# Attention with decay and a squared-relu feed-forward on one core: the order of all engines from a list scheduler, the first tokens in pairs, free choice of engine, weight quarters between the loads

## The chip, the cores and the metric

One core of one Trainium2 chip. The metric is the device time of one execution in microseconds (us). Engines are named TensorE (PE in the profile; its weight loads are PEld), VectorE (DVE), ScalarE (ACT), GpSimd (POOL) and SyncE (SP, which issues loads and stores here). Runs of one kernel can show steps of 0.6 to 1.7% that mostly, but not always, go with the granted TensorE clock (in one set of runs the kernel before took 218.1 to 218.2 us at 0.989 to 0.991 and 219.5 to 220.0 at 0.983 and 0.984); each comparison below is therefore made between runs taken together, on one chip, and where runs at other times are compared their ratios to the kernel before are used.

## The reference

```python
B, H, S, D = 4, 8, 768, 48          # d_model = H*D = 384, d_ff = 2048
for t in range(S):                   # decayed linear attention
    cur = einsum('bhd,bhe->bhde', u * k[t], v[t])
    y[t] = einsum('bhd,bhde->bhe', r[t], state + cur)
    state = w * state + einsum('bhd,bhe->bhde', k[t], v[t])
x = y as (B*S, H*D)                  # 3072 tokens
g = relu(x @ w_in) ** 2
out = g @ w_out
```

Both kernels cut the 768 steps into six chunks of 128, so that there are 24 *blocks* (chunk by batch) of 128 tokens.

## The kernel before

In the cuts and profiles below, `hps` (`ps_h` in the changed kernel) is a result of the first feed-forward product and `ops` (`ps_o`) one of the second. Per block, attention needs five elementwise *products* of 128x384 (`kpad = k*wk`, `rpad = r*wr`, `rk = r*k`, `rku = rk*u`, `dv = v*du`) and, from the second chunk on, a sixth (`sm*wc`). All run on GpSimd.

```python
def prep(n):
    nc.gpsimd.tensor_tensor(kp[:, :, :D], kt, wk, ALU.mult)       # kpad
    nc.gpsimd.tensor_tensor(rp[:, :, :D], rt, wr, ALU.mult)       # rpad
    nc.scalar.copy(vb, vt)
    nc.gpsimd.tensor_tensor(rk, rt, kt, ALU.mult)
    nc.gpsimd.tensor_tensor(rku, rk, ub, ALU.mult)
def du(n):  nc.vector.tensor_reduce(q["du"], q["rku"], axis=X, op=ALU.add)
def dv(n):  nc.gpsimd.tensor_tensor(q["dv"], q["vb"], du broadcast, ALU.mult)
# s1: transposes of kp, rp -> rkT;  k^T v -> state sm;  state_end: sm *= wc (GpSimd)
# s2: at = k r^T, masked on VectorE -> AT;  s3: y -> yb (VectorE);  s4: transpose -> xt
...
def m1(c, f):                          # one of 16 column tiles of a chunk of four blocks
    for kk in range(NK): nc.tensor.matmul(out=hps, lhsT=w_in_sb[...], rhs=xts[c][:, kk]...)
    nc.vector.tensor_scalar(gr, hps, 0.0, None, ALU.max)                    # relu
    nc.scalar.activation(gs[c][:, f]..., gr, AF.Square)                     # square
def m2(c, b, part):                    # a quarter of one block's second product
    for f in range(part * 4, part * 4 + 4): nc.tensor.matmul(out=ops, lhsT=gs[c][:, f, b, :], rhs=w_out_sb[:, f, :], ...)
    ...
for slot in range(-2, NU + 2 * B):     # the fixed order
    at(slot + 1, dv); at(slot + 2, prep)
    if slot == 1: all four w_in quarters are loaded
    if 3 <= slot < 7: one w_out quarter is loaded
    at(slot + 1, s1); moe(0); at(slot, s3); moe(1)
    at(slot + 1, state_end); at(slot + 1, s2); moe(2); at(slot, s4); moe(3)
    at(slot + 2, du); load(slot + 5)
    # moe(part): m1 of the chunk one behind, m2 of the chunk two behind
```

Of the kernel before, what the change touches and what calls it, by code (L numbers as in the profile page):

```python
# [15 lines left out]
def kernel(  # L16
# [23 lines left out]
    NU = NCH * B  # L40

    const = ctx.enter_context(tc.tile_pool(name="const", bufs=1))
    lpool = ctx.enter_context(tc.tile_pool(name="loads", bufs=5))
    apool = ctx.enter_context(tc.tile_pool(name="attn", bufs=3))
    xpool = ctx.enter_context(tc.tile_pool(name="xg", bufs=2))
    mpool = ctx.enter_context(tc.tile_pool(name="moe", bufs=4))
    aps = ctx.enter_context(tc.tile_pool(name="attn_psum", bufs=3, space=bass.MemoryType.PSUM))
    hps_pool = ctx.enter_context(tc.tile_pool(name="h_psum", bufs=3, space=bass.MemoryType.PSUM))
    ops_pool = ctx.enter_context(tc.tile_pool(name="o_psum", bufs=2, space=bass.MemoryType.PSUM))
# [7 lines left out]
    wcol = const.tile([128, NP], F32)  # L57
    nc.vector.memset(wcol, 1.0)
    with nc.allow_non_contiguous_dma(reason="384 decay values, one column a head"):
        for i in range(2):  # L60
            nc.scalar.dma_start(
                out=wcol[i * PAD : i * PAD + D, :],
                in_=bass.AP(tensor=w.tensor, offset=w.offset + i * D, ap=[[1, D], [2 * D, NP]]),
            )
    ub = const.tile([128, H, D], F32)
    nc.scalar.dma_start(
        out=ub, in_=bass.AP(tensor=u.tensor, offset=u.offset, ap=[[0, 128], [1, HD]])
    )

    loads = {}  # L70

    def load(n):
        c, b = divmod(n, B)
        t0 = c * C
        tiles = []
        for nm, src in (("kt", k), ("rt", r), ("vt", v)):
            t = lpool.tile([C, H, D], F32, name=nm)
            nc.sync.dma_start(out=t, in_=src[b, :, t0 : t0 + C, :].rearrange("h t d -> t h d"))
            tiles.append(t)
        loads[n] = tiles  # L80

    NAHEAD = 5
    for n in range(NAHEAD):
        load(n)

# [5 lines left out]
    def load_w_in(q):  # L91
        fs = slice(q * dff // 4, (q + 1) * dff // 4)
        nc.gpsimd.dma_start(out=w_in_sb[:, :, fs], in_=w_in_v[:, :, fs])  # L93

    def load_w_out(q):
        fs = slice(q * NF // 4, (q + 1) * NF // 4)
        nc.gpsimd.dma_start(out=w_out_sb[:, fs, :], in_=w_out_v[:, fs, :])


    iota_i = const.tile([128, 1], mybir.dt.int32)  # L100
    nc.gpsimd.iota(iota_i, pattern=[[0, 1]], base=0, channel_multiplier=1)
    er = const.tile([128, 1], F32)
    nc.vector.tensor_scalar(er, iota_i, 1.0, float(-MID), ALU.mult, ALU.add)
    ek = const.tile([128, 1], F32)
    nc.vector.tensor_scalar(ek, iota_i, -1.0, float(MID - 1), ALU.mult, ALU.add)
    identb = const.tile([128, 128], BF16)
    make_identity(nc, identb)
    smask = const.tile([128, 128], F32)
    make_upper_triangular(nc, smask, val=1.0, diag=False)

    NPADS = 3
    rpads, kpads = [], []
    for i in range(NPADS):
        rp = const.tile([C, H, PAD], BF16, name=f"rpad{i}")
        kp = const.tile([C, H, PAD], BF16, name=f"kpad{i}")
        nc.vector.memset(rp, 0.0)
        nc.vector.memset(kp, 0.0)
        rpads.append(rp)
        kpads.append(kp)


    lnw = const.tile([128, HD], F32)
    nc.scalar.activation(lnw, wb, AF.Ln)
    lnc = const.tile([128, NP], F32)
    nc.scalar.activation(lnc, wcol, AF.Ln)
    wk = const.tile([128, H, D], F32)
    nc.scalar.activation(wk.rearrange("p h d -> p (h d)"), lnw, AF.Exp, scale=ek)  # L127
    wr = const.tile([128, H, D], F32)
    nc.scalar.activation(wr.rearrange("p h d -> p (h d)"), lnw, AF.Exp, scale=er)
    wcs = const.tile([128, NP], F32)  # L130
    nc.scalar.activation(wcs, lnc, AF.Exp, scale=float(C))
    wc = const.tile([128, NP, 2, D], F32)
    nc.vector.memset(wc, 0.0)
    for i in range(2):
        rows = slice(i * PAD, i * PAD + D)
        nc.vector.tensor_copy(wc[rows, :, i, :], wcs[rows, :, None].to_broadcast([D, NP, D]))

    states = {b: None for b in range(B)}
    stb = {b: None for b in range(B)}
    xts, gs = {}, {}  # L140
    unit = {}

    def prep(n):
        kt, rt, vt = loads.pop(n)
        rp, kp = rpads[n % NPADS], kpads[n % NPADS]
        nc.gpsimd.tensor_tensor(kp[:, :, :D], kt, wk, ALU.mult)  # L146
        nc.gpsimd.tensor_tensor(rp[:, :, :D], rt, wr, ALU.mult)  # L147
        vb = apool.tile([C, H, D], BF16, name="vb", bufs=4)
        nc.scalar.copy(vb, vt)  # L149
        rk = apool.tile([C, H, D], F32, name="rk")  # L150
        nc.gpsimd.tensor_tensor(rk, rt, kt, ALU.mult)  # L151
        rku = apool.tile([C, H, D], F32, name="rku")
        nc.gpsimd.tensor_tensor(rku, rk, ub, ALU.mult)  # L153
        unit[n] = dict(rp=rp, kp=kp, vb=vb, rku=rku)

    def du(n):
        q = unit[n]
        q["du"] = apool.tile([C, H], F32, name="du")
        nc.vector.tensor_reduce(q["du"], q["rku"], axis=mybir.AxisListType.X, op=ALU.add)  # L159

    def dv(n):
        q = unit[n]
        q["dv"] = apool.tile([C, H, D], F32, name="dv")
        nc.gpsimd.tensor_tensor(q["dv"], q["vb"], q["du"][:, :, None].to_broadcast([C, H, D]), ALU.mult)  # L164

    def s1(n):
        c, b = divmod(n, B)
        q = unit[n]
        rk_p = aps.tile([128, NP, 2, C], BF16, name="rk_p", tag="a")
        kv_p = None  # L170
        if c < NCH - 1:
            kv_p = aps.tile([128, NP, 2, D], F32, name="kv_p", tag="a")
        for p in range(NP):
            nc.tensor.transpose(rk_p[:, p, 1, :], q["kp"][:, 2 * p : 2 * p + 2, :], identb)  # L174
        for p in range(NP):
            nc.tensor.transpose(rk_p[:, p, 0, :], q["rp"][:, 2 * p : 2 * p + 2, :], identb)  # L176
        rkT = apool.tile([128, NP, 2, C], BF16, name="rkT")
        nc.scalar.copy(rkT, rk_p)  # L178
        q["rkT"] = rkT
        q["st"] = stb[b]  # L180
        if kv_p is not None:
            for p in range(NP):
                nc.tensor.matmul(
                    out=kv_p[:, p], lhsT=q["kp"][:, 2 * p : 2 * p + 2, :],
                    rhs=q["vb"][:, 2 * p : 2 * p + 2, :], start=True, stop=True,
                )
            sm = apool.tile([128, NP, 2, D], F32, name=f"sm{b}", bufs=2)
            if c == 0:
                nc.vector.tensor_tensor(sm, kv_p, wc, ALU.mult)
            else:  # L190
                nc.vector.tensor_tensor(sm, kv_p, states[b], ALU.add)
            states[b] = sm

    def state_end(n):
        c, b = divmod(n, B)
        if c == NCH - 1:
            return
        sm = states[b]
        if c > 0:
            nc.gpsimd.tensor_tensor(sm, sm, wc, ALU.mult)  # L200
        sb = apool.tile([128, NP, 2, D], BF16, name=f"sb{b}", bufs=2)
        nc.scalar.copy(sb, sm)
        stb[b] = sb

    def s2(n):
        q = unit[n]
        rkT = q["rkT"]
        at = [aps.tile([128, NP, C], F32, name=f"at_p{i}", tag="a") for i in range(2)]
        for p in range(NP):
            for i in range(2):  # L210
                rows = slice(i * PAD, i * PAD + D)
                nc.tensor.matmul(  # L212
                    out=at[i][:, p, :], lhsT=rkT[rows, p, 1, :], rhs=rkT[rows, p, 0, :],
                    start=True, stop=True,
                )
        AT = apool.tile([128, 2, NP, C], BF16, name="AT")
        for i in range(2):
            nc.vector.tensor_tensor(
                AT[:, i], at[i], smask[:, None, :].to_broadcast([128, NP, C]), ALU.mult
            )  # L220
        q["AT"] = AT

    def s3(n):
        c, b = divmod(n, B)
        q = unit[n]
        y_p = aps.tile([128, NP, 2, D], F32, name="y_p", tag="a")
        for p in range(NP):
            if c > 0:
                nc.tensor.matmul(  # L229
                    out=y_p[:, p], lhsT=q["rkT"][:, p, 0, :], rhs=q["st"][:, p],  # L230
                    start=True, stop=False, skip_group_check=True,
                )
            for i in range(2):
                nc.tensor.matmul(  # L234
                    out=y_p[:, p, i, :], lhsT=q["AT"][:, i, p, :], rhs=q["vb"][:, 2 * p + i, :],
# [49 lines left out]
    def at(n, fn):  # L285
        if 0 <= n < NU:
            fn(n)
# [59 lines left out]
```

## Time and profile before

| | before |
|---|---|
| median time, three runs | 220.02 us (219.78 to 220.11) |
| profiled span | 217.1 us |
| TensorE, VectorE, ScalarE, GpSimd busy | 174.7, 133.2, 120.5, 135.4 us |
| first feed-forward matmul (hps) | 45.3 us |

The first fence is from the page of the kernel before: busy time of each engine, then its span in 40 slices, with the busy share of a slice in tenths.

```profile
PE 174.7 (80%) x1480; PEld 101.9 (47%) x1480; DVE 133.2 (61%) x224; ACT 120.5 (55%) x219; POOL 135.4 (62%) x153
...
PE   0135543467578499998999989999999999999993
...
DVE  4245551429758588887787887787777775555200
...
POOL 2488898997996949787888779687687200000000
```

The averages hide two stages. In the first third GpSimd has 8s and 9s while TensorE has 3s to 7s; from about 75 us (slice 14) TensorE has 9s. The next fence is the windows view of the kernel before: for each stretch its length, then busy us (and instructions) of each engine, the granted clock, the DMA share and GB/s.

```profile
core 0: us, PE busy (x) PEld busy (x) DVE busy (x) ACT busy (x) POOL busy (x), PEclk, DMA share, GB/s
20.00:40.00 20.00, 10.04 (x100) 6.88 (x97) 9.37 (x17) 6.73 (x11) 18.28 (x21) 1.00 1.00 175
40.00:60.00 20.00, 12.11 (x108) 6.53 (x106) 11.98 (x22) 8.81 (x17) 18.12 (x21) 1.00 0.99 168
...
80.00:100.00 20.00, 20.00 (x189) 11.99 (x188) 16.40 (x27) 13.72 (x26) 16.11 (x18) 1.00 0.50 107
...
120.00:140.00 20.00, 19.40 (x179) 11.56 (x177) 15.62 (x27) 13.63 (x26) 15.95 (x18) 1.00 0.53 116
```

From 20 to 60 us GpSimd is busy for 36.4 of 40 us, TensorE for 22. From 80 us TensorE is full. The chain of waits of the kernel before (start, length, who) says what one block costs in the first stage:

```profile
9.60 1.01 POOL rpad_137 L147
10.60 0.98 POOL rk L151
...
11.65 1.00 POOL rku L153
...
12.68 0.56 DVE du L159
...
13.37 0.83 POOL dv L164
14.20 0.95 POOL kpad_142 L146
```

Five products on GpSimd and one wait for `du` make 5.5 us a block. The group of such a product, from the page (busy us and mean ns of one after the bar), follows:

```profile
L151 POOL TENSOR_TENSOR rk<-rt,kt 128x384 f32<-128x384 f32 x24 | 23.9, 997 | 0.0
```

### The profile page before, as it was taken

The numbers are of one execution on the slowest core, as the hardware profiler recorded it, in microseconds if no ns is written. First come the engines' busy times: TensorE is split into PE (matmuls) and PEld (weight loads), VectorE is DVE, ScalarE is ACT, GpSimd is POOL, SyncE is SP. The second block draws the span as 40 slices with busy tenths as digits, with TensorE's granted clock in tenths as the row PEclk, the third lists the DMA queues.
The fourth block names the chain that finished last, engine by engine and source line by source line (L and its number), as shares of the span: only waits on it lengthen the run. The fifth ranks groups of instructions, "written<-read, shape, count | busy, mean of one in ns | idle before, by whom it ended". The sixth has DMA issues, their size and how long they took to land.

```text
span 217.1 us, 3956 instructions
## 1 busy us (share of the span) xinstructions
PE 174.7 (80%) x1480; PEld 101.9 (47%) x1480; DVE 133.2 (61%) x224; ACT 120.5 (55%) x219; POOL 135.4 (62%) x153
## 2 busy tenths in 40 slices
PE   0135543467578499998999989999999999999993
PEld 0123332324334255565566655665555555555551
DVE  4245551429758588887787887787777775555200
ACT  3544441057268565866677666866767655555410
POOL 2488898997996949787888779687687200000000
PEclk9999999999979999999999999999999999999998
DMA  5999969999665006346652565536610100111022
GB/s 101 195 199 209 202 119 191 208 175 179 124 104 72 3 0 145 73 100 120 149 120 69 105 145 118 120 78 126 145 41 36 36 35 15 53 48 38 36 72 72
DMA packets 82771, 22.67 MB, mean 104 GB/s; under 512 B 75840, under 2 KB 82752, under 8 KB 82752
## 3 DMA queue, kind: packets, MB, share of 16 engines
q1 hardware_dynamic: 78480, 19.08, 41.1%
q0 software_dynamic: 3712, 3.15, 9.7%
q10 hardware_dynamic: 560, 0.20, 0.4%
q8 instruction: 11, 0.18, 0.3%
q14 instruction: 8, 0.07, 0.1%
HBM read 20.84 MB, written 4.72 MB: 118 GB/s over the span
## 4 chain that ended last, share of the span: by engine, by line
PE 65%; POOL 23%; ACT 3%; DVE 3%; DMA 2%; issue 2%; POOLq 0%; ACTq 0%
PE ops L275 29%; PE hps L259 26%; POOL rku L153 4%; POOL rk L151 4%; POOL dv L164 3%; DMA wcol<-in_w_dram 2%; PE y_p L234 2%; DVE du L159 1%; PE y_p L229 1%; PE rk_p L176 1%; PE rk_p L174 1%; POOL w_in_sb L93 1%; POOL rpad_137 L147 1%; POOL rpad_145 L147 1%; POOL rpad_141 L147 1%
## 5 line engine op out<-in xcount | busy, mean ns | idle before, releaser
L259 PE MATMUL hps<-xt,w_in_sb 128*128 128x512 bf16 x288 | 80.5, 389 | 8.1 <-ACT xt L252 8.1
L265 DVE TENSOR_SCALAR gr<-hps 128x512 f32<-128x512 f32 x96 | 65.8, 688 | 33.7 <-PE hps L259 24.2
L275 PE MATMUL ops<-w_out_sb,g 128*128 128x384 bf16 x384 | 75.5, 326 | 0.0
L266 ACT ACTIVATE g<-gr 128x512 bf16<-128x512 f32 x96 | 59.8, 632 | 27.2 <-DVE gr L265 26.6
L275 PEld LDWEIGHTS <-g 128*128 128x128 bf16 x384 | 37.5, 98 | 33.4
L164 POOL TENSOR_TENSOR dv<-vb,du 128x384 f32<-128x384 bf16 x24 | 19.9, 829 | 26.8 <-DVE du L159 25.2
L259 PEld LDWEIGHTS <-w_in_sb 128*128 128x128 bf16 x288 | 23.8, 99 | 25.0 <-issue 9.9
L178 ACT COPY rkT<-rk_p 128x1024 bf16<-128x1024 bf16 x24 | 24.4, 1015 | 7.3 <-PE rk_p L176 7.3
L153 POOL TENSOR_TENSOR rku<-rk,ub 128x384 f32<-128x384 f32 x24 | 23.9, 996 | 1.9
L159 DVE TENSOR_REDUCE du<-rku 128x8 f32<-128x384 f32 x24 | 13.1, 547 | 18.0 <-POOL rku L153 17.8
L151 POOL TENSOR_TENSOR rk<-rt,kt 128x384 f32<-128x384 f32 x24 | 23.9, 997 | 0.0
L239 DVE TENSOR_TENSOR yb<-y_p,dv 128x384 bf16<-128x384 f32 x24 | 13.3, 554 | 6.1 <-PE y_p L234 6.1
L281 ACT COPY osb<-ops 128x384 f32<-128x384 f32 x24 | 11.2, 466 | 7.9 <-PE ops L275 6.4
L212 PEld LDWEIGHTS <-rkT 48*128 48x128 bf16 x192 | 6.5, 101 | 18.6 <-ACT rkT L178 9.6
L149 ACT CAST vb<-vt 128x384 bf16<-128x384 f32 x24 | 12.3, 513 | 2.3 <-DMA vt<-in_v_dram 2.3
L234 PEld LDWEIGHTS <-AT 128*128 128x128 bf16 x192 | 10.5, 103 | 5.5 <-issue 4.4
L252 ACT COPY xt<-yt_p 128x384 bf16<-128x384 bf16 x24 | 11.1, 462 | 2.1 <-PE yt_p L251 2.1
L234 PE MATMUL y_p<-vb,AT 128*128 128x48 bf16 x192 | 12.1, 191 | 0.0
L146 POOL TENSOR_TENSOR kpad_138<-kt,wk 128x384 bf16<-128x384 f32 x8 | 8.0, 996 | 6.7 <-ACT wk L127 6.7
L174 PE MATMUL rk_p<-identb,kpad_138 128*128 128x128 bf16 x32 | 3.5, 240 | 10.3 <-POOL kpad_138 L146 9.7
L251 PE MATMUL yt_p<-identb,yb 128*128 128x128 bf16 x72 | 8.8, 237 | 0.0
L229 PEld LDWEIGHTS <-rkT 128*128 128x128 bf16 x80 | 7.7, 98 | 1.7 <-issue 0.3
(224 smaller groups left out, 210.7 us busy)
## 6 DMA issues: line engine op xcount, KB each, us to landing
kt<-in_k_dram SPq DMA_DIRECT2D x24, 192.0 KB, 3.5
rt<-in_r_dram SPq DMA_DIRECT2D x24, 192.0 KB, 3.7
vt<-in_v_dram SPq DMA_DIRECT2D x24, 192.0 KB, 3.8
out_dram<-osb SPq DMA_DIRECT2D x24, 192.0 KB, 1.9
w_in_sb<-in_moe_w_in_dram POOLq DMA_DIRECT2D x4, 384.0 KB, 8.6
w_out_sb<-in_moe_w_out_dram POOLq DMA_DIRECT2D x4, 384.0 KB, 5.9
wb<-in_w_dram SPq DMA_DIRECT2D x1, 192.0 KB, 3.6
ub<-in_u_dram ACTq DMA_DIRECT2D x1, 192.0 KB, 5.7
```

The source lines that it names most:

```text
L149: nc.scalar.copy(vb, vt)
L151: nc.gpsimd.tensor_tensor(rk, rt, kt, ALU.mult)
L153: nc.gpsimd.tensor_tensor(rku, rk, ub, ALU.mult)
L159: nc.vector.tensor_reduce(q["du"], q["rku"], axis=mybir.AxisListType.X, op=ALU.add)
L164: nc.gpsimd.tensor_tensor(q["dv"], q["vb"], q["du"][:, :, None].to_broadcast([C, H, D]), ALU.mult)
L178: nc.scalar.copy(rkT, rk_p)
L234: nc.tensor.matmul(out=y_p[:, p, i, :], lhsT=q["AT"][:, i, p, :], rhs=q["vb"][:, 2 * p + i, :], start=(c == 0), stop=True, skip_group_chec ...
L239: nc.vector.tensor_tensor(yb, y_p.rearrange("t p i d -> t (p i d)"), q["dv"].rearrange("t h d -> t (h d)"), ALU.add)
L259: nc.tensor.matmul(out=hps, lhsT=w_in_sb[:, kk, f * 128 : (f + 1) * 128], rhs=xts[c][:, kk].rearrange("p b t -> p (b t)"), start=(kk == 0) ...
L265: nc.vector.tensor_scalar(gr, hps, 0.0, None, ALU.max)
L266: nc.scalar.activation(gs[c][:, f].rearrange("p b t -> p (b t)"), gr, AF.Square)
L275: nc.tensor.matmul(out=ops, lhsT=gs[c][:, f, b, :], rhs=w_out_sb[:, f, :], start=(f == 0), stop=(f == NF - 1),)
```

## The change

The intent is to fill TensorE before 75 us. Every operation becomes an object with its possible engines, assumed durations, dependencies and buffers; a list scheduler repeatedly places the operation that can start first, and the kernel is emitted in that order. Feed-forward starts after two blocks instead of four (pairs for the first four blocks). Products may run on GpSimd or VectorE, relu on VectorE or ScalarE, squares on ScalarE or GpSimd. The weight quarters are issued between the first blocks.

```diff
+    op({"P": 1.0, "V": 0.47}, K + 2, [q["rk"]], two(lambda e, T=T: e.tensor_tensor(T("rku"), T("rk"), ub, ALU.mult)), ...)
+    op({"P": 1.0, "V": 0.47}, K + 0.1, ...)     # kp;  the same for rp, dv ("P": 0.83) and sm*wc; rk on P alone
     [...]
+    groups = [[0, 1], [2, 3]] + [list(range(i, i + B)) for i in range(B, NU, B)]
+    W_IN_AT, W_OUT_AT = (0, 1, 1, 2), (3, 4, 5, 6)
     [...]
+    o_r = op({"V": 0.14 + 0.1375 * L, "A": 0.2 + 0.1 * L}, key - 1, [o_m], relu, uses=[gr, h])
+    o_sq.append(op({"A": 0.22 + 0.1 * L, "P": 0.333 * L}, key - 1, [o_r], square, uses=[gr, g]))
     [...]
+    while left:                                  # the list scheduler
+        for o in left:
+            t = latest end (+ latency) of its dependencies and of the old users of the buffers it takes
+            for e in o.eng:
+                s = max(t, free[e])
+                rank = (s, o.key + (AWAY if e is not the home engine else 0))
+        place the lowest rank; free[e] = s + o.eng[e]
+    for o in placed: o.emit(o.by)
-    for slot in range(-2, NU + 2 * B): [...]     # the fixed order
     [...]
-    wcs = Exp(128 * lnc) on ScalarE              # decay of a chunk, from a one-column load (0.8 KB, 5.0 us)
+    seven times: nc.vector.tensor_tensor(sq, wcs, wcs, ALU.mult)   # 128x4, on VectorE
```

In the schedule that results, 46 of the 136 products are on VectorE (13 `rku`, 10 `kp`, 13 `rp`, 8 `dv`, 2 `sm`), 34 of 112 relus on ScalarE and 27 of 112 squares on GpSimd.

## The prediction

> **What bounds the kernel now.** The span is 217.1 us (median time 220.02, so 2.9 us lie outside it). The chain of waits gives TensorE 65% and GpSimd 23%; the windows show two stages. Until about 72 us GpSimd is the limit (9.1, 9.2, 18.1 us busy in 20-30, 30-40, 40-60), while TensorE has 5 of every 10 us. The chain there runs kpad, rpad, rk, rku, dv at 5.5 us a token block (later 6.5 to 8). The first feed-forward matmul starts at 45.3 us, after four blocks. From 75 us TensorE is full: 6.78 us a block (85.47 to 92.25 in the chain): four hps triples at 0.64, four ops quadruples at 0.65, about 1.6 of attention. The end is 68 ops matmuls (11.2 us) and a 3.5 us tail.
>
> **What the change does.** TensorE work hardly changes (48 hps matmuls of 512 columns become 96 of 256): 6.78 us x 24 blocks, less small parts, is 161 us. The gain must come from filling TensorE before 75 us. The order listing shows:
> - Feed-forward starts after two blocks instead of four; ops matmuls begin in block 5's time instead of block 8's.
> - 46 of 136 attention products go from GpSimd to VectorE; GpSimd gets 27 of 112 squares (20 wide, estimated 1.33 us each from 1.0 for 384 columns); ScalarE takes 34 of 112 relus.
> - My sums from trace durations (moved product estimated 0.5 us): GpSimd 135 -> 125, VectorE 133 -> 146, ScalarE 120 -> 139.
> - Weight quarters are issued from block 0 on, not at 29 us. Loads arrive every 2.9 us a block; the eight quarters took 9.7% of the span, 21 us of all engines. Eight blocks plus weights need about 45 us of DMA either way.
>
> **The sum.** Pair 0's hps start at about 20 us (blocks 0 and 1 through, first quarter landed), 4.5 us of TensorE work done. Then 157 us of it plus 3.5 tail: span 180.5 if never idle. I add:
> - 7 us between 20 and 55, where VectorE, ScalarE and GpSimd together are about 94% loaded (76 of 81 us), weights compete with loads, and TensorE runs at half rate at times. [...] the trace agrees (an hps triple 1.44 us at 45.3, 0.81 at 48.9).
> - 3 us for products on VectorE. [...]
> - 3 us of order misses in the steady part.
>
> The three overlap (some 2.5 us less): span 191, plus 2.9 outside: **194 us** (186 to 204). Faster by over 2%: 0.97; within 2%: 0.025; slower: 0.005.
>
> **What would show it.** First hps at 18-23 us; TensorE near full from 55 us, not 75; block spacing still 6.7-7.0 us there; GpSimd under 70% busy; moved products longer than 0.55 us on average when GpSimd is busy; last tail unchanged.
>
> **What would make it wrong.** [...] the fixed order, built on modelled times, meeting late loads or weights and stalling in-order engines (200+); or the early stage running TensorE full from 25 us (under 187).

The sum came to 194 us: 180.5 if TensorE never idles, plus 7, 3 and 3, less 2.5 of overlap, plus 2.9 outside the span. Two stand as estimates alone: the 3 us, and the part of the 7 us that is slow matmuls. For these "half rate" is the word: the trace of the kernel before shows an hps triple of 1.44 us at 45.3 and one of 0.82 us at 48.9, 1.8 times. The 0.5 us of a moved product is an estimate too; `du` and `yb`, which read 128x384 elements on VectorE, took 0.55 us each in the kernel before.

## The result, and the profile after

| | before | after |
|---|---|---|
| median time, four runs each | 219.9 us (219.75 to 220.11) | 206.27 us (206.07 to 206.49) |
| profiled span | 217.1 us | 204.0 us |
| TensorE, VectorE, ScalarE, GpSimd busy | 174.7, 133.2, 120.5, 135.4 us | 175.2, 153.5, 127.6, 126.3 us |
| mean granted clock | 0.989 | 0.971 |

The ratio is 0.938 (95% interval 0.9363 to 0.9396). Ratios here and below are the mean time of one kernel's fast runs over that of the other's of the same rounds, so not quite the ratio of the medians quoted. The change gained 13.6 us; 26 had been predicted. Busy times and slices, from the page of the changed kernel (PEclk is the granted TensorE clock in tenths):

```profile
PE 175.2 (86%) x1529; PEld 106.4 (52%) x1529; DVE 153.5 (75%) x260; ACT 127.6 (63%) x240; POOL 126.3 (62%) x136
...
PE   0147893999599999977999999799999999999992
...
DVE  4899689478859999899989999999764564455200
...
POOL 2767489548899698999998899995322020422200
PEclk9999999589969999999999999999999999999998
```

TensorE indeed fills earlier. But VectorE, 75% busy in the mean, now has 8s and 9s from slice 12 to slice 27, and TensorE has 7s in the middle of what had been its full stage. The windows view of the changed kernel:

```profile
20.00:40.00 20.00, 14.97 (x125) 10.07 (x127) 15.35 (x29) 11.49 (x28) 13.67 (x18) 0.88 1.13 194
40.00:60.00 20.00, 17.21 (x176) 12.31 (x177) 15.78 (x30) 12.68 (x30) 15.29 (x18) 0.86 0.49 74
...
80.00:100.00 20.00, 17.46 (x179) 10.46 (x177) 19.49 (x33) 15.93 (x30) 19.25 (x19) 1.00 0.96 199
100.00:120.00 20.00, 19.74 (x192) 11.34 (x190) 19.10 (x32) 15.82 (x32) 18.31 (x18) 1.00 0.54 115
120.00:140.00 20.00, 18.88 (x173) 10.81 (x170) 19.97 (x33) 15.80 (x29) 17.93 (x17) 1.00 0.09 32
```

From 80 to 140 us VectorE is busy for 58.6 of 60 us, and TensorE idles for 3.9. The chain of waits of the changed kernel runs through VectorE there:

```profile
87.37 0.50 DVE rku L217
87.86 1.27 DVE kp_79 L220
89.14 0.46 DVE du L228
89.60 0.81 DVE rp_76 L223
...
94.28 1.34 DVE dv L231
```

The pieces differ oddly: `rku` takes 0.50 us and `kp`, of the same size, 1.27. The groups of the changed kernel, by form:

```profile
L214 POOL TENSOR_TENSOR rk<-rt,kt 128x384 f32<-128x384 f32 x24 | 27.3, 1144 | 4.5 <-DVE wsq L171 4.0 <-DVE rku L217 0.5
...
L217 DVE TENSOR_TENSOR rku<-rk,ub 128x384 f32<-128x384 f32 x13 | 9.7, 746 | 0.7 <-POOL rk L214 0.7
...
L231 DVE TENSOR_TENSOR dv<-vb,du 128x384 f32<-128x384 bf16 x8 | 7.8, 971 | 0.2
...
L223 DVE TENSOR_TENSOR rp_75<-rt,wr 128x384 bf16<-128x384 f32 x3 | 5.8, 1932 | 0.0
...
L220 DVE TENSOR_TENSOR kp_79<-kt,wk 128x384 bf16<-128x384 f32 x4 | 3.9, 968 | 0.0
```

Summed over all their groups, the 46 moved products took 44.4 us of VectorE, 0.97 each, almost the 1.0 us that they had cost on GpSimd. `rk`, which stayed on GpSimd, grew from 0.997 to 1.144 us. The timeline of the changed kernel (start, length, engine, operation) shows one of them:

```profile
32.01 0.83 POOL L231 TENSOR_TENSOR dv<-vb,du 128x384 f32<-128x384 bf16 x1
...
32.57 2.59 DVE L223 TENSOR_TENSOR rp_75<-rt,wr 128x384 bf16<-128x384 f32 x1
...
32.80 0.99 POOL L220 TENSOR_TENSOR kp_78<-kt,wk 128x384 bf16<-128x384 f32 x1
...
33.75 0.99 POOL L214 TENSOR_TENSOR rk<-rt,kt 128x384 f32<-128x384 f32 x1
...
35.09 0.55 DVE L321 TENSOR_TENSOR yb<-ps_a,dv 128x384 bf16<-128x384 f32 x1
```

The VectorE product is recorded from 32.57 to 35.16. Three GpSimd products follow each other until 34.74; it ends 0.42 us after the last of them. `yb` behind it, which reads one operand from PSUM, takes 0.55 us.

That product is the extreme. The usual case, from the same view of the same run:

```profile
87.41 1.31 POOL L223 TENSOR_TENSOR rp_75<-rt,wr 128x384 bf16<-128x384 f32 x1
...
87.79 1.35 DVE L220 TENSOR_TENSOR kp_79<-kt,wk 128x384 bf16<-128x384 f32 x1
...
88.68 1.31 POOL L214 TENSOR_TENSOR rk<-rt,kt 128x384 f32<-128x384 f32 x1
```

`kp_79` ends 0.42 us after the GpSimd product that was running, and the next GpSimd product, recorded as starting meanwhile, takes 1.31 us instead of 1.00. Of the 46 moved products 17 took 0.54 to 0.58 us; each of the other 29 ended 0.41 to 0.43 us after a GpSimd operation, and only two of them sat through more than one.

### The profile page after: what moved, and what is told of

Same layout as the page of the kernel before. It is cut to its first block, busy times and chain, and to the rows that moved or that the text cites. A ratio compares the mean times of both kernels' runs of the same rounds, so it can differ in the third digit from the quotient of the medians.

```text
span 204.0 us, 4084 instructions
## 1 busy us (share of the span) xinstructions
PE 175.2 (86%) x1529; PEld 106.4 (52%) x1529; DVE 153.5 (75%) x260; ACT 127.6 (63%) x240; POOL 126.3 (62%) x136
## 4 chain that ended last, share of the span: by engine, by line
PE 66%; DVE 20%; DMA 6%; issue 3%; POOL 3%; ACT 1%; POOLq 0%; DVEq 0%; ACTq 0%
PE ps_o L396 27%; PE ps_h L363 26%; DMA w_out_sb<-in_moe_w_out_dram 4%; PE ps_a L241 4%; DVE AT L298 3%; PE ps_a L288 3%; PE ps_a L313 2%; DMA wrow<-in_w_dram 2%; DVE rku L217 2%; DVE gr L374 2%; PE ps_a L331 2%; PE ps_a L308 2%; DVE dv L231 2%; DVE rp_75 L223 1%; DVE yb L321 1%
## 5 line engine op out<-in xcount | busy, mean ns | idle before, releaser
L374 DVE TENSOR_SCALAR gr<-ps_h 128x512 f32<-128x512 f32 (+1 forms) x78 | 46.7, 609 | 26.4 <-PE ps_h L363 21.9
L298 DVE TENSOR_TENSOR AT<-ps_a,smask 128x512 bf16<-128x512 f32 x48 | 30.9, 679 | 2.7 <-PE ps_a L288 2.4
L247 ACT COPY rkT<-ps_a 128x1024 bf16<-128x1024 bf16 x24 | 24.2, 1010 | 6.1 <-PE ps_a L241 6.1
L376 ACT ACTIVATE gr<-ps_h 128x512 f32<-128x512 f32 (+1 forms) x34 | 17.8, 532 | 8.0 <-PE ps_h L363 7.6
L404 ACT COPY osb<-ps_o 128x384 f32<-128x384 f32 x24 | 11.4, 475 | 15.2 <-PE ps_o L396 15.0
L321 DVE TENSOR_TENSOR yb<-ps_a,dv 128x384 bf16<-128x384 f32 x24 | 13.1, 548 | 2.0 <-PE ps_a L313 2.0
L313 PE MATMUL ps_a<-vb,AT 128*128 128x48 bf16 x192 | 12.6, 190 | 1.5 <-DVE AT L298 1.5
L363 PE MATMUL ps_h<-xt_1214,w_in_sb 128*128 128x512 bf16 x48 | 12.5, 379 | 1.2 <-DVE gr L374 1.2
L288 PE MATMUL ps_a<-rkT 48*128 48x128 bf16 x192 | 10.7, 233 | 3.1 <-ACT rkT L247 3.1
L396 PE MATMUL ps_o<-w_out_sb,g_2035 128*128 128x384 bf16 x64 | 13.0, 326 | 0.0
L396 PE MATMUL ps_o<-w_out_sb,g_1046 128*128 128x384 bf16 x64 | 12.9, 326 | 0.0
L396 PE MATMUL ps_o<-w_out_sb,g_2479 128*128 128x384 bf16 x64 | 12.9, 326 | 0.0
L363 PE MATMUL ps_h<-xt_2112,w_in_sb 128*128 128x512 bf16 x48 | 12.8, 379 | 0.0
L363 PE MATMUL ps_h<-xt_2535,w_in_sb 128*128 128x512 bf16 x48 | 12.8, 379 | 0.0
L363 PE MATMUL ps_h<-xt_1707,w_in_sb 128*128 128x512 bf16 x48 | 12.7, 380 | 0.0
L396 PE MATMUL ps_o<-w_out_sb,g_1578 128*128 128x384 bf16 x64 | 12.5, 326 | 0.0
```

The lines of the kernel that those rows point to most:

```text
L247: lambda e, T=T, rk_p=rk_p: nc.scalar.copy(T("rkT"), rk_p.tile),
L288: nc.tensor.matmul(out=ts[i][:, p, :], lhsT=T("rkT")[rows, p, 1, :], rhs=T("rkT")[rows, p, 0, :], start=True, stop=True,)
L298: lambda e, T=T, i=i, x=x: nc.vector.tensor_tensor(T("AT")[:, i], x.tile, smask[:, None, :].to_broadcast([128, NP, C]), ALU.mult),
L313: nc.tensor.matmul(out=t[:, p, i, :], lhsT=T("AT")[:, i, p, :], rhs=T("vb")[:, 2 * p + i, :], start=st is None, stop=True, skip_group_chec ...
L321: lambda e, T=T, y_p=y_p: nc.vector.tensor_tensor(T("yb"), y_p.tile.rearrange("t p i d -> t (p i d)"), T("dv").rearrange("t h d -> t (h d) ...
L363: nc.tensor.matmul(out=t, lhsT=w_in_sb[:, kk, f * 128 : (f + 1) * 128], rhs=xt.tile[:, kk].rearrange("p b t -> p (b t)"), start=(kk == 0), ...
```

## The experiments

Theory A: a VectorE product with two SBUF inputs and a GpSimd operation exclude each other, and in this change the waiting is on the path. Theory B: the path was lost elsewhere, namely in the late `w_out` quarters (TensorE's chain waits for the first one from 30.6 to 37.9 us) and in a fixed order made from modelled times. "In its own order" means that the schedule was left as it is and only the emitted instruction exchanged.

### one_input: the same order without the second input

```diff
+        class OneInput:
+            def tensor_tensor(out, in0, in1, op):
+                nc.vector.tensor_reduce(out, in0[..., None], axis=X, op=ALU.add)   # sum over one element
-        two = lambda f: (lambda e: f({"P": nc.gpsimd, "V": nc.vector}[e]))
+        two = lambda f: (lambda e: f({"P": nc.gpsimd, "V": OneInput}[e]))
```

> The changed kernel in its own order, but each of the 46 products moved to VectorE is replaced by a one-input VectorE operation (a sum over one element) of the same size; results wrong on purpose. Theory A (mutual exclusion of two-input VectorE products and GpSimd is what ate the missing 12 us): the 46 operations fall from 44 us to 22-26 us, GpSimd's rk from 1.14 to 1.00 us, and the time falls to 194-200 us. Rival B (late w_out quarters and the fixed order are the cause, VectorE's extra busy time is off the path): the operations get short but the time stays at 204-206 us.

Measured: 197.43 us (196.45 to 201.35; two of six runs slow), ratio 0.9002 (0.8943 to 0.906); results wrong. The changed kernel's ratio is 0.938, so the second input costs 0.038 of 219.5 us, 8.3 us. Groups of one_input:

```profile
L220 POOL TENSOR_TENSOR rk<-rt,kt 128x384 f32<-128x384 f32 x24 | 23.8, 1000 | 5.1 <-DMA rt<-in_r_dram 4.4 <-DVE rku L216 0.7
...
L216 DVE TENSOR_REDUCE rku<-rk 128x384 f32<-128x384 f32 x13 | 7.1, 547 | 1.6 <-POOL rk L220 1.6
L216 DVE TENSOR_REDUCE rp<-rt 128x384 bf16<-128x384 f32 x13 | 7.0, 544 | 0.1
```

The 46 operations take 25.1 us in all (0.55 each), so 19.3 us of the 44.4 had been waiting; `rk` is back at 1.000 us, and GpSimd's busy time falls from 126.3 to 117.0 us, so GpSimd had waited as well. Windows of one_input (its profiled run was a slow one):

```profile
80.00:100.00 20.00, 19.92 (x198) 11.56 (x196) 18.69 (x36) 17.71 (x34) 18.91 (x21) 1.00 0.97 199
100.00:120.00 20.00, 20.00 (x200) 12.25 (x199) 17.71 (x34) 16.29 (x32) 17.57 (x19) 1.00 0.52 110
120.00:140.00 20.00, 20.00 (x192) 11.82 (x191) 17.86 (x33) 15.80 (x29) 14.91 (x16) 1.00 0.09 32
```

TensorE's idle time from 80 to 140 us falls from 3.9 to 0.1 us (0.1 as well in `both` below, which was profiled in a fast run). Theory A holds, with order and instruction count the same; "the exclusion" below means this waiting as it was measured here, and no run shows what is behind it. The stand-in drops no wait for another engine: the second input is a constant or, for `dv`, the `du` that VectorE itself computed before. One rival is not separated: the fast runs of one_input had a mean granted clock of 0.991 to 0.999, those of the change 0.971 to 0.981. Some 0.02 of 200 us is 4 us at most (estimate from these figures), so a part of the 8.3 us may have come by way of the clock; no run holds it fixed.

### wout_early: the w_out quarters one place earlier

```diff
+    em = [o.emit for o in gos]        # gos: the eight weight issues on GpSimd
+    gos[3].emit = lambda e: (em[3](e), em[4](e))     # first w_out quarter right behind the last w_in quarter
+    gos[4].emit, gos[5].emit, gos[6].emit, gos[7].emit = em[5], em[6], em[7], lambda e: None
```

> The changed kernel in its own order, but each w_out quarter is issued one place earlier on GpSimd (the first right behind the last w_in quarter, at about 22 us instead of 30.6; the last at 41 instead of 52). Theory B (the first ops matmul's 7.3 us wait for the first w_out quarter, 30.6 to 37.9, is lost time): 200-203 us, first ops matmul at 32-34 us. Rival A [...]: within 1 us of 206. Rival D (DMA is full until 40 us, so an earlier quarter only makes the loads behind it later): first ops matmul earlier, but time 205-207 us.

Measured: 207.08 us (206.81 to 207.26), ratio 0.9457 (0.9409 to 0.9504), correct. Nothing is gained. The first quarter landed at 31.4 us instead of 37.9, yet the first ops matmul started at 37.97 us, as in the change (37.92; 32 to 34 had been expected). In the chain VectorE took the place of the weights: from 30.3 to 36.3 us it runs through `rku`, `du`, the masks, an `rp` that took 2.58 us beside GpSimd, and `yb`. The two waits had covered each other. Later the chain waits 4.5 us for a load of `vt` (from 44.1 us), as rival D had it.

### both

Both edits together.

> Both edits at once (one-input stand-ins, results wrong on purpose, and w_out quarters one place earlier). If A and B are separate costs the gains add: 191-197 us, what was predicted for the change. If one hides the other, the time is that of the better one alone, within 1 us.

Measured: 196.53 us (194.31 to 196.8), ratio 0.8954 (0.8888 to 0.902). Against one_input's 0.9002 that is 0.5% at most, inside the intervals. The late quarters are worth next to nothing even without the exclusion (first ops matmul at 36.9 us, 37.3 in one_input). So the half of theory B that concerns the weights falls; its other half, the fixed order, is answered only by the windows of one_input, and only from 80 to 140 us.

### pool_only: a correct kernel without the moves

```diff
-        op({"P": 1.0, "V": 0.47}, ...)        # rku, kp, rp, sm; likewise dv
+        op({"P": 1.0}, ...)
```

The scheduler then makes a new order.

> A correct kernel: the products may run on GpSimd alone, as before the change; the list schedule is made anew, all else as changed. Theory A: VectorE's products go (44 us of its time), GpSimd gets 46 us more work and no exclusion, its busy time about 155-165 us; the time is no worse than 206 and may be 200-205, as the move bought nothing. If the move was worth its price: GpSimd again bounds the first 60 us and the time is 208-214 us.

Measured: 199.22 us (197.16 to 200.61, two of four runs slow), ratio 0.9021 (0.8949 to 0.9093), correct. GpSimd's busy time is 143.9 us (155 to 165 had been expected: the scheduler took 17 squares away from it in return; a square took it 1.04 us for 512 columns and 0.61 for 256, so 1.7 ns for each further column). Giving GpSimd the products back makes the kernel 8 us faster than the change; its fast runs (197.2 and 197.9 us) lie below the 200 to 205 us expected.

### old_rp_vector and old_rp_one_input: one product moved in the kernel before

```diff
-        nc.gpsimd.tensor_tensor(rp[:, :, :D], rt, wr, ALU.mult)
+        nc.vector.tensor_tensor(rp[:, :, :D], rt, wr, ALU.mult)                      # old_rp_vector
+        nc.vector.tensor_reduce(rp[:, :, :D], rt[..., None], axis=X, op=ALU.add)     # old_rp_one_input
```

> The kernel before with one single edit: the product rpad is computed on VectorE instead of GpSimd; correct, program order kept. GpSimd bounds its first 72 us at 5.5 us a block, VectorE is half idle there. Theory A (exclusion): the product occupies VectorE for more than 0.7 us on average, and as GpSimd cannot work beside it a block shortens by at most 0.5 us: time 213-218 us. Rival (no exclusion; then a move is worth the full 1.0 us a block): 206-211 us and products of 0.5 us.

> The same edit on the kernel before, but rpad is a one-input VectorE operation of the same size (results wrong on purpose). Theory A: 0.55 us each, and the block gains the whole 1.0 us: 206-211 us, at least 4 us below the two-input version. Rival: the same time as the two-input version, within 1.5 us.

Measured: 212.88 us (212.46 to 213.18), ratio 0.9714 (0.9677 to 0.9752), correct; and 209.14 us (207.95 to 210.26), ratio 0.9527 (0.9465 to 0.9589), wrong. Groups of old_rp_vector:

```profile
L164 POOL TENSOR_TENSOR dv<-vb,du 128x384 f32<-128x384 bf16 x24 | 23.9, 995 | 39.1 <-DVE du L159 39.1
...
L147 DVE TENSOR_TENSOR rpad<-rt,wr 128x384 bf16<-128x384 f32 x24 | 18.2, 760 | 0.0
```

Group of old_rp_one_input:

```profile
L148 DVE TENSOR_REDUCE rpad<-rt 128x384 bf16<-128x384 f32 x24 | 13.0, 543 | 0.0
```

The two-input product takes 0.76 us instead of 0.54, and `dv` on GpSimd 0.995 instead of 0.829: each side waits for the other. (Three of the 24 products waited, 1.34 to 3.66 us in all; the other 21 took 0.54 to 0.55, and `dv` took 1.01 behind most of them.) The second input costs 1.9%, 4.1 us by the ratios, in the old program order as well; the runs at equal granted clock, 0.984, differ by only 2.3 us (212.46 and 212.64 against 210.26 and 210.06). And yet the move gains 6 us there, in a kernel whose first stage is bound by GpSimd with VectorE half idle: a move is not bad as such. (212.88 us lies 0.1 below the range expected.)

### fours and fixed_engines: where the gain comes from

On top of pool_only, either groups of four from the start, or every relu on VectorE and every square on ScalarE:

```diff
-    groups = [[0, 1], [2, 3]] + [...]
+    groups = [list(range(i, i + B)) for i in range(0, NU, B)]              # fours
-    {"V": 0.14 + 0.1375 * L, "A": ...} and {"A": 0.22 + 0.1 * L, "P": ...}
+    {"V": 0.14 + 0.1375 * L}           and {"A": 0.22 + 0.1 * L}           # fixed_engines
```

> The scheduled kernel with products on GpSimd alone and, in addition, without pairs: feed-forward groups of four blocks from the start. If the pairs are what fills TensorE early, as predicted (first hps at 20 instead of 45 us): the first hps comes at 35-38 us and the time is 4-9 us above that of the pairs (202-208 us). If the order and the weights alone do it: within 2 us of 198.

> The scheduled kernel with products on GpSimd alone and, in addition, every relu on VectorE and every square on ScalarE, as before the change; pairs and order kept. If the free choice of engine for relu and square matters in the early, vector-bound stage: 200-206 us. If not: within 1.5 us of 198.

Measured: fours 200.2 us (199.98 to 201.06), ratio 0.9144 (0.9106 to 0.9182); fixed_engines 198.87 us (197.72 to 199.3), ratio 0.9068 (0.9024 to 0.9112); both correct. Against pool_only (0.9021, and 0.9006 when repeated below) the pairs are worth about 1.3% and the free engine choice at most 0.6%. The first hps of fours starts at 34.2 us, of pool_only at 23.4, of the kernel before at 45.3. For fours 202 to 208 us and a first hps at 35 to 38 us had been expected; the pairs were worth less than that. So most of the gain over the kernel before is in what these kernels have in common, the new order, the earlier weights and the other way to the decay column, which were not separated further.

### early_only and late_only, with both kernels repeated

```diff
+        both = lambda p: {"P": p, "V": 0.47} if n < 8 else {"P": p}      # early_only; late_only: n >= 8
```

> The changed kernel once more, on the same chip as the next three: 205.5-207 us.

> The scheduled kernel with products on GpSimd alone, once more, on the same chip: 197-200.5 us, so 6-9 us below the changed kernel.

> Products may go to VectorE for the first 8 token blocks only (15 do), for the other 16 they stay on GpSimd; correct. If the exclusion costs its time where VectorE is full (60 to 140 us), as the windows say, and the first stage, bound by GpSimd, even gains from giving some products away: 195-199 us, at or below products on GpSimd alone. If the harm is done in the first stage: 201-206 us.

> The reverse: products may go to VectorE from block 8 on only (34 do), the first 8 blocks keep theirs on GpSimd; correct. If the harm lies in 60 to 140 us: 201-207 us, with VectorE over 95% busy from 80 to 140. If it lies in the first stage: 197-200 us.

| same chip | median us | ratio to before (95%) |
|---|---|---|
| after_again | 207.97 (204.59 to 209.41, four of six slow) | 0.9398 (0.9311 to 0.9485) |
| pool_only_again | 197.5 (196.67 to 197.86) | 0.9006 (0.8963 to 0.905) |
| early_only | 203.03 (201.56 to 203.43) | 0.9256 (0.9212 to 0.9301) |
| late_only | 207.87 (206.52 to 210.99) | 0.9472 (0.942 to 0.9523) |

All are correct. pool_only is again 0.039 of 219.2 us, 8.6 us, faster than the change. The expectation for early_only failed: moves in the first eight blocks alone cost 5.5 us too. They were few (15), but the five `rp` took 0.98 to 2.59 us, and the two longest (2.59 and 1.85) lie on the chain of waits. Their group in early_only:

```profile
L224 DVE TENSOR_TENSOR rp<-rt,wr 128x384 bf16<-128x384 f32 x5 | 8.1, 1622 | 0.0
```

late_only lost 10 us, no less than the change with moves everywhere. From 40 to 60 us TensorE is busy for only 11.8 of 20 us in its profile, and one product lies on the chain there (timeline):

```profile
51.12 5.43 DVE L221 TENSOR_TENSOR kp<-kt,wk 128x384 bf16<-128x384 f32 x1
```

It sat through six GpSimd operations in a row, and TensorE stood idle for 6.6 us until the `yb` behind it. How much of the 10 us is due to this one wait no run shows. From 80 to 140 us VectorE was 94% busy, less than the 95% expected. As these two were scheduled anew, their losses need not add up, and they do not.

### one_input_early and one_input_late: the same split in the order of the change

```diff
-        two = lambda f: (lambda e: f({"P": nc.gpsimd, "V": OneInput}[e]))
+        two = lambda f, n=n: (lambda e: f({"P": nc.gpsimd, "V": OneInput if n < 8 else nc.vector}[e]))   # late: n >= 8
```

> The changed kernel in its own order, one-input stand-ins only for products of token blocks 0 to 7 (15 of the 46; results wrong on purpose). If the cost is paid where VectorE is full, from 60 to 140 us: within 2 us of the changed kernel (204-208 us). If the first stage pays as much: 201-204 us, 3 us or more below it.

> The reverse, stand-ins only for blocks 8 to 23 (31 of the 46; results wrong on purpose). If the cost is paid from 60 to 140 us: 198-202 us, TensorE full from 80 to 140 us. If in the first stage: 203-206 us. The two gains should add up to the 8-9 us of all stand-ins, within 2 us.

Measured: one_input_early 207.77 us (205.71 to 207.94), ratio 0.9451 (0.9407 to 0.9494); one_input_late 202.81 us (201.56 to 203.62), ratio 0.9238 (0.92 to 0.9277). Freeing the first eight blocks alone brings nothing against the change (0.938 and 0.940); freeing the others brings about 1.5%; freeing all brings 4%. The gains are not additive, so that expectation failed, and one_input_late lies just above its 198 to 202 us. A reading that fits the windows, but that no run isolates: while VectorE is the full engine from 80 to 140 us (58.6 of 60 us in one_input_early as well), arriving there earlier buys nothing; once TensorE is full there instead, each us gained in the first stage counts.

### act_squares and act_squares_no_g: the tiny squares

The seven 128x4 squares of the decay column are two-input VectorE products as well. The timeline of pool_only_again:

```profile
5.90 7.23 DVE L171 TENSOR_TENSOR wsq<-wsq 128x4 f32<-128x4 f32 x7
...
6.23 1.00 POOL L214 TENSOR_TENSOR rk<-rt,kt 128x384 f32<-128x384 f32 x1 [3.96 <-DMA rt<-in_r_dram]
...
7.18 0.99 POOL L220 TENSOR_TENSOR kp<-kt,wk 128x384 bf16<-128x384 f32 x1
...
13.80 0.56 DVE L268 TENSOR_TENSOR sm<-ps_a,wc 128x384 f32<-128x384 f32 x1
```

Seven operations on four columns hold VectorE for 7.2 us, and the first state product starts only at 13.8 us. Two took 0.16 us before GpSimd had begun; the next three took 0.92 to 0.95 each, one GpSimd product apiece; the sixth took 3.76, through a weight issue and three products. It is not always so: in the first profile of pool_only the seven took 3.4 us, and the copies of `wc` behind them 4.1.

```diff
-            nc.vector.tensor_tensor(sq, wcs, wcs, ALU.mult)
+            nc.scalar.activation(sq, wcs, AF.Square)            # act_squares, on top of pool_only
-    {"A": 0.22 + 0.1 * L, "P": 0.333 * L}
+    {"A": 0.22 + 0.1 * L}                                       # act_squares_no_g, in addition
```

(act_squares also issues the two exponentials of `wk` and `wr` on ScalarE ahead of the squares, outside the scheduler's order; the cut leaves this out.)

> Products on GpSimd alone, and the seven squares of the decay column (128x4 elements) on ScalarE instead of VectorE; correct. If they wait for GpSimd's products: they fall from 7.2 us in all to under 2.5 us, the state product sm0 starts before 11.5 us instead of 13.8, and the time falls by 1-3 us, to 194.5-197 us. If their 7.2 us have another reason or are off the path: within 0.7 us of 197.5.

> As act_squares, and no feed-forward square on GpSimd (10 were); correct. GpSimd is the fullest vector engine before 140 us, so the early stage could gain 0-2 us; ScalarE gets 6 us more, which could cost as much. 194-198 us.

Measured: act_squares 199.6 us (197.52 to 201.2), ratio 0.9052 (0.9004 to 0.91); act_squares_no_g 197.81 us (195.77 to 199.16), ratio 0.8993 (0.8947 to 0.9039); both correct. The squares fall to 1.4 us in all and in act_squares the first state product starts at 11.49 us, as expected (13.28 in act_squares_no_g, where the `wc` copies waited instead); but the time does not fall. What was freed there seems to be off the path: in the profile of act_squares the chain goes through the loads until 23.5 us (SyncE's queue 7%, `vt` 4% of the span). Neither differs from pool_only beyond the intervals, so pool_only stays the version that beats both kernels: 197.5 us.

## Why the prediction was wrong

- Right: what bounded the kernel before, and that the gain must come from filling TensorE early. The first hps came at 22.3 us (18 to 23 predicted), GpSimd is 62% busy (under 70), the moved products took 0.97 us in the mean (over 0.55), the tail is as before (64 ops matmuls in 10.5 us), and the sign of the change was right.
- Wrong, and the failed step: "3 us for products on VectorE". That these products could cost far more and make VectorE critical had been named as a risk (cut above, as is the estimate of the waiting). VectorE waited 19.3 us, 0.42 a product; the 9.3 us that GpSimd waited came on top. The failure is where this falls: it is not mostly off the path. Replacing the second input in an unchanged order gave 8.3 us back, and keeping the products on GpSimd 8.6; so the term is 8 to 9 us instead of 3 (with what may come by way of the clock). Against a span of some 190 us, the predicted 146 us of VectorE and 19 us of waiting leave slack; but the work is not spread over the span. The last moved product starts at 142.4 us, and from 80 to 140 VectorE ran at 98%. What the traces show of the exclusion: 0.97 us in the mean for a two-input product beside GpSimd, 0.55 for a one-input operation of the same size and order, and each product that waited ended 0.41 to 0.43 us after a GpSimd operation.
- The second term that was too small: without the exclusion the sum was 194 - 3 = 191 us (up to 193.5, as the terms overlap), and the change without it, one_input, took 197.4 (`both` 196.5). Some 4 to 6 us remain. The early stage does not hold them: in `both` TensorE is busy for 30.1 of the 35 us from 20 to 55, where the sum had 35 - 7 = 28, and full from 55 on, as predicted. From there to the end it is busy for 135.7 us, where the sum leaves 157 - 28 = 129. So the work of TensorE, 161 us in the sum and 172.0 us of busy time in `both`, was too small; which part of it (stretches of slower matmuls, attention, gaps between matmuls) no run separates.
- "3 us of order misses in the steady part": with the exclusion gone TensorE idles 0.1 us from 80 to 140. The order itself missed nearly nothing there.
- Named as risks and not the cause: late weights (wout_early, both). The slow matmuls of the 7 us are not explained: the granted clock was 0.88 and 0.86 in the mean from 20 to 60 us in the change, but in the kernel before it is recorded as 1.00 from 20 to 60 us, where TensorE is busy for only 22 of 40 us, although an hps triple there took 1.44 us at 45.3 and 0.82 at 48.9. No run tested the clock by itself.

## What to carry to other kernels

Before moving a two-input elementwise operation from GpSimd to VectorE, count it on both: where the two met here, one waited for the other (29 of 46 products on VectorE, 11 of 24 `rk` on GpSimd), so one engine's relief was a wait on the other, and a scheduler that models them as independent does not see it. Nor was the wait of one length: 27 of those 29 sat through one GpSimd operation only, and the GpSimd operation behind took up to 1.35 us instead of 1.0; but one sat through two (1.86 us), one through three (2.59 us, ended 0.42 us after the third), one in late_only through six (5.43 us), and one 128x4 square through a weight issue and three products (3.76 us). What decides this, no run shows. Engine load alone does not say whether the move pays. It gained 6 us in the kernel before, where GpSimd was full and VectorE half idle; in the first blocks of the new kernel, where GpSimd was as full (39.1 of 40 us from 20 to 60 in pool_only_again) and VectorE busy for 26.5, it cost 5.5 us (early_only, a new schedule, with two products that waited long on its chain). Compare engine load with the stage in which it has to be done, not with the span, and test a long wait in the chain by taking it away: the 7 us wait for a weight quarter was worth nothing, as another wait lay beside it.
